# Single load buffers, the second batch's q transposed by DMA, and projections moved next to score bursts, in a Linformer attention with a gated feed-forward layer

## The chip, the cores and the metric

The kernel runs on one core of one Trainium2 chip. The metric is device microseconds of one launch, the median of several runs. The span is the time from the first to the last instruction in a profile of one of them, and the granted clock is the share of full speed at which TensorE was allowed to run. All runs told of here are of the fast state. Engines are named as in the profile: PE (TensorE), DVE (VectorE), ACT (ScalarE), POOL (GpSimd, which issues the loads here) and SP (SyncE, which issues stores and DMA transposes).

## The reference

Eight batches of eight heads, 1024 tokens, head size 64; keys and values are projected along the sequence to 64 rows, then softmax attention, then a feed-forward layer on 8192 tokens of width 512 with 2048 hidden units.

```python
k_proj = np.einsum('ks,bhsd->bhkd', E, k)
v_proj = np.einsum('ks,bhsd->bhkd', F, v)
scores = np.matmul(q, k_proj.transpose(0, 1, 3, 2)) / np.sqrt(64)
attn = softmax(scores)                    # over 64 columns
x = np.matmul(attn, v_proj)               # then (B, H, S, D) -> (B*S, H*D)
h = x @ w_in
out = (h * sigmoid(1.702 * h)) @ w_out
```

## The kernel before

The output is made in 16 blocks of 512 tokens, two a batch. In each block PE first runs 16 slots of `ffn1` (four matmuls each), then 8 slots of `ffn2` (eight matmuls each, named O to O+7). Attention work for later blocks is placed at fixed slots with `at(block, slot, ...)`: the projection of k and v of a batch, score bursts (four small matmuls of q with the projected k), and normalisation bursts. `qT` and `kt` are the transposed q and the transposed projected k that the scores read; `vq` is the projected v. The program fixes the order of the instructions itself (`manual_schedule`), so each engine has them in the order in which they are written; waits are put in where data or buffers ask for them. The listing is abridged.

```python
ldpool = ctx.enter_context(tc.tile_pool(name="ldpool", bufs=2))   # k, v, q as loaded

def load(b):                        # all on one in-order queue (POOL)
    load_kv(k, kt, b, "k_sb")
    if b == 1: load_kv(v, vt, b, "v_sb")
    load_q(b)                       # 8 pieces
    if b > 1:  load_kv(v, vt, b, "v_sb")

def proj(b):      # 16 matmuls in pairs: k into one half of a PSUM bank, v into the other
    ...
def kv_out(b):    # DVE copies k_b and the two vq; for b > 1 SP transposes k_b into kt by DMA
    ...
def q_tr(b, g):   # q on PE: 8 transposes, then one DVE copy    (batches 0 and 1)
    ...
def q_dma(b):     # q by one DMA transpose of 1 MB on SP        (batches 2 to 7)
    ...
# cut: prologue, four(), scores(), norm(), tok(), x_tr(), ffn1(), ffn2()
at(1, 4, proj(1)); at(1, 5, kv_out(1))
at(1, 7, lambda: k_tr(1, kbs[1], 0), q_dma(2))
for g in range(4):
    at(1, 8 + 2 * g, q_tr(1, g))
for b in range(2, B):
    j = max(2, NB2 * b - 3)         # NB2 = 2
    at(j, 2, proj(b)); at(j, 3, kv_out(b))
    if b > 2: at(NB2 * b - 4, O, q_dma(b))
for j in range(3, NBLK - 2):        # the bursts: scores and normalisation
    for u in range(2):
        if j + 3 < NBLK: at(j, O + 5 * u, scores(j + 3, u))
        at(j, O + 5 * u, norm(j + 2, u))
```

The softmax here doesn't subtract the row's maximum and nothing guards it: scores larger than these inputs give would overflow.

## Time and profile before

| | before |
|---|---|
| time, median of the first three runs | 518.31 us |
| span of the profiled run | 516.5 us, clock 1.000 |
| PE / DVE / ACT busy | 98% / 49% / 51% |
| start of block 1, 2, 3, 4 on PE (timeline) | 55.86, 91.14, 124.26, 156.25 us |
| last PE matmul starts | 512.64 us |

The prediction below shows the lines that carry the reading: PE is never idle after the first 22 us, so only what PE does, or waits for, sets the time. Starts are compared below rather than ends, because the ends of pipelined matmuls are modelled.

### The profile page before, as it was taken

The numbers are of one execution on the slowest core, as the hardware profiler recorded it, in microseconds if no ns is written. First come the engines' busy times: TensorE is split into PE (matmuls) and PEld (weight loads), VectorE is DVE, ScalarE is ACT, GpSimd is POOL, SyncE is SP. The second block draws the span as 40 slices with busy tenths as digits, with TensorE's granted clock in tenths as the row PEclk, the third lists the DMA queues.
The fourth block names the chain that finished last, engine by engine and source line by source line (L and its number), as shares of the span: only waits on it lengthen the run. The fifth ranks groups of instructions, "written<-read, shape, count | busy, mean of one in ns | idle before, by whom it ended". The sixth has DMA issues, their size and how long they took to land.

```text
span 516.5 us, 6729 instructions
## 1 busy us (share of the span) xinstructions
PE 506.9 (98%) x2856; PEld 233.2 (45%) x2856; DVE 251.4 (49%) x231; ACT 264.0 (51%) x439; POOL 77.4 (15%) x96
## 2 busy tenths in 40 slices
PE   6899999999999999999999999999999999999997
PEld 3584454444444444444444444444444444444444
DVE  3533324766774672818547282655818275560000
ACT  1575464555646456474555645465473646344351
POOL 6442620821510024000510000000000000000000
PEclk9999999999999999999999999999999999999999
DMA  9999999999996039550694201060200101010102
GB/s 162 197 203 207 217 180 182 165 191 159 241 152 162 1 90 166 106 133 0 147 176 121 53 41 48 0 164 0 84 4 1 81 1 81 1 82 1 81 1 82
DMA packets 113950, 53.78 MB, mean 104 GB/s; under 512 B 87680, under 2 KB 111488, under 8 KB 112000
## 3 DMA queue, kind: packets, MB, share of 16 engines
q0 software_dynamic: 84384, 29.37, 50.2%
q1 hardware_dynamic: 29456, 23.73, 16.6%
q8 instruction: 22, 0.36, 0.3%
q10 hardware_dynamic: 80, 0.26, 0.1%
q14 instruction: 8, 0.07, 0.0%
HBM read 59.24 MB, written 16.78 MB: 147 GB/s over the span
## 4 chain that ended last, share of the span: by engine, by line
PE 94%; DMA 4%; POOL 1%; issue 0%; DVE 0%; DVEq 0%; POOLq 0%
PE f_ps L333 43%; PE f_ps L301 42%; PE f_ps L144 3%; DMA w_in_sb<-in_moe_w_in_dram 2%; DMA v_sb<-in_v_dram 2%; PE f_ps L225 2%; PE d_ps L225 1%; PE n_ps L225 1%; PE f_ps L325 1%; PE n_ps L287 0%; PE d_ps L272 0%; PE f_ps L208 0%; POOL k_sb L57 0%; PE f_ps L205 0%; POOL q_sb L57 0%
## 5 line engine op out<-in xcount | busy, mean ns | idle before, releaser
L259 DVE RECIPROCAL rden<-d_ps 128x512 f32<-128x512 f32 x52 | 174.4, 3353 | 149.0 <-PE d_ps L225 149.0
L301 PE MATMUL f_ps<-xT,w_in_sb 128*128 128x512 bf16 (+1 forms) x1088 | 228.4, 367 | 0.2
L333 PE MATMUL f_ps<-w_out_sb,gT 128*128 128x512 bf16 x1008 | 227.0, 379 | 0.0
L304 ACT ACTIVATE gT<-f_ps 128x512 bf16<-128x512 f32 (+1 forms) x268 | 153.7, 575 | 85.4 <-PE f_ps L301 84.4
L301 PEld LDWEIGHTS <-w_in_sb 128*128 128x128 bf16 x1088 | 104.5, 98 | 116.4 <-issue 4.3
L333 PEld LDWEIGHTS <-gT 128*128 128x128 bf16 x1008 | 95.7, 98 | 120.4 <-issue 11.1
L336 ACT COPY o_sb<-f_ps 128x512 f32<-128x512 f32 x63 | 37.0, 587 | 133.5 <-PE f_ps L333 123.7
L63 POOL DMA_DIRECT2D q_sb<-in_q_dram x56 | 49.1, 894 | 67.5 <-DMA k_sb<-in_k_dram 27.7
L239 ACT ACTIVATE expT<-f_ps 128x512 bf16<-128x512 f32 (+1 forms) x68 | 35.2, 574 | 14.4 <-PE f_ps L225 14.4
L260 DVE TENSOR_TENSOR xT<-n_ps,rden 128x512 bf16<-128x512 f32 x52 | 36.0, 692 | 5.4
L327 DVE COPY o_sb<-f_ps 128x256 f32<-128x256 f32 x1 | 0.4, 424 | 50.9 <-PE f_ps L325 50.9
L57 POOL DMA_DIRECT2D k_sb<-in_k_dram x9 | 7.8, 864 | 103.7 <-PE f_ps L144 101.4
L239 ACT ACT_TABLE_LOAD x13 | 16.7, 1283 | 4.7 <-PE f_ps L225 4.5
L243 ACT ACT_TABLE_LOAD x14 | 18.0, 1283 | 0.3
L225 PE MATMUL f_ps<-qT,kt 64*64 64x512 bf16 (+1 forms) x136 | 13.8, 386 | 0.4 <-ACT expT L239 0.4
L144 PE MATMUL f_ps<-k_sb,eft 128*64 128x512 bf16 x56 | 13.4, 382 | 0.0
L144 PE MATMUL f_ps<-v_sb,eft 128*64 128x512 bf16 x56 | 13.4, 382 | 0.0
L211 DVE COPY qT<-f_ps 128x1024 bf16<-128x1024 bf16 x8 | 5.5, 692 | 12.4 <-PE f_ps L205 6.8
L277 DVE RECIPROCAL rd<-d_ps 128x4 f32<-128x4 f32 x22 | 3.8, 175 | 15.5 <-PE d_ps L272 15.4
L225 PEld LDWEIGHTS <-kt 64*64 64x64 bf16 x136 | 4.0, 103 | 14.3 <-issue 14.3
L225 PE MATMUL d_ps<-expT,ones 64*64 64x512 bf16 x104 | 10.2, 381 | 0.0
L225 PE MATMUL n_ps<-expT,vq 64*64 64x512 bf16 x104 | 10.0, 376 | 0.0
(57 smaller groups left out, 127.0 us busy)
## 6 DMA issues: line engine op xcount, KB each, us to landing
out_dram<-o_sb SPq DMA_DIRECT2D x15, 1024.0 KB, 4.5
k_sb<-in_k_dram POOLq DMA_DIRECT2D x7, 1024.0 KB, 13.5
v_sb<-in_v_dram POOLq DMA_DIRECT2D x7, 1024.0 KB, 10.7
q_sb<-in_q_dram POOLq DMA_DIRECT2D x56, 128.0 KB, 11.1
w_in_sb<-in_moe_w_in_dram POOLq DMA_DIRECT2D x8, 256.0 KB, 12.7
w_out_sb<-in_moe_w_out_dram POOLq DMA_DIRECT2D x4, 512.0 KB, 14.7
k_sb<-in_k_dram POOLq DMA_DIRECT2D x2, 512.0 KB, 8.0
out_dram<-o_sb SPq DMA_DIRECT2D x3, 256.0 KB, 2.0
```

The lines of the kernel that those rows point to most:

```text
L57: nc.gpsimd.dma_start(out=dst[b][:, h:h + n, js:js + jn], in_=sv[:, h:h + n, js:js + jn])
L63: nc.gpsimd.dma_start(out=qt[b][:, j], in_=qv[:, j])
L144: nc.tensor.matmul(kvps[b][r], eft[:, j, e * KP:(e + 1) * KP], (kt, vt)[e][b][:, :, j, :], start=(j == 0), stop=(j == J - 1))
L225: nc.tensor.matmul(outs[i][r], lhsTs[i][ri], rhss[i][ri], start=True, stop=True)
L239: nc.scalar.activation(expT[h][:, 2 * u + i, ts], s_ps[i], AF.Exp, scale=scale)
L243: nc.scalar.preload_act_table(AF.Gelu_apprx_sigmoid)
L259: nc.vector.reciprocal(rden, d_ps[i])
L260: nc.vector.tensor_tensor(x_of(h)[:, 2 * u + i, :], n_ps[i], rden, op=ALU.mult)
L301: nc.tensor.matmul(h_ps, w_in_sb[:, kc, fc * P:(fc + 1) * P], xT[j][:, kc, ts], start=(kc == 0), stop=(kc == KC - 1))
L304: nc.scalar.activation(gts[j][:, fc, ts], h_ps, AF.Gelu_apprx_sigmoid)
L333: nc.tensor.matmul(o_ps[n], gts[j][:, fc, n * P:(n + 1) * P], w_out_sb[:, fc, :], start=(fc == 0), stop=(fc == FC - 1))
L336: nc.scalar.copy(osb[j][:, n, :], o_ps.pop(n))
```

## The change

Its intent: PE no longer transposes q of batch 1, two half-size DMA transposes do; k, v and q have one buffer each, so that batch 2 is loaded only once batch 1 is used up and does not run beside those transposes; from batch 4 on the projection sits directly ahead of a burst, so that the array leaves its full tiling once instead of twice.

```diff
-    ldpool = ctx.enter_context(tc.tile_pool(name="ldpool", bufs=2))
+    ldpool = ctx.enter_context(tc.tile_pool(name="ldpool", bufs=1))
...
-    def q_dma(b):
+    def q_dma(b, j0=0, n=J):           # a part of q
...
     (prologue: tok(0, 0..1) ahead of the second v projection, x_tr spread out)
...
-    at(1, 4, proj(1))
-    at(1, 5, kv_out(1))
-    at(1, 7, lambda: k_tr(1, kbs[1], 0), q_dma(2))
-    for g in range(4):
-        at(1, 8 + 2 * g, q_tr(1, g))
+    at(1, 10, proj(1))
+    at(1, 11, kv_out(1))
+    at(1, 13, lambda: k_tr(1, kbs[1], 0))
+    at(1, 1, q_dma(1, 0, JB), q_dma(1, JB, JB))
...
+    at(1, O + 7, q_dma(2))
+    at(2, 2, proj(2))
+    at(2, 3, kv_out(2))
+    for b in range(3, B):
+        j = NB2 * b - 4
+        at(j, O, q_dma(b))
+        at(j, O + 6, proj(b), kv_out(b))
...
-                at(j, O + 5 * u, scores(j + 3, u))
-            at(j, O + 5 * u, norm(j + 2, u))
+                at(j, O + 6 * u, scores(j + 3, u))
+            at(j, O + 6 * u, norm(j + 2, u))
...
-            at(j, O + 6, gelu_table)
+            at(j, O + 7, gelu_table)
```

More of the change, by code (lines that the diff above doesn't have):

```diff
@@ L53, in load_kv @@
         if b not in dst:
-            dst[b] = ldpool.tile([P, H, J, D], BF16, name=name, bufs=1 if name == "q0_sb" else 2)
+            dst[b] = ldpool.tile([P, H, J, D], BF16, name=name)
         sv = src[b].rearrange("h (p j) d -> p h j d", p=P)
@@ L200, in go @@
             for jj in range(2):
-                j = 2 * g + jj
-                if b == 0:
-                    for h in range(H):
-                        r = h % 2 * D
-                        nc.tensor.transpose(t_ps[r:r + D, jj, h // 2, :], qt[0][:, h, j, :], ident)
-                else:
-                    for p in range(HP):
-                        nc.tensor.transpose(
-                            t_ps[:, jj, p, :],
-                            qt[b][:, j, 2 * p:2 * p + 2, :].rearrange("s t d -> s (t d)"), ident)
+                for h in range(H):
+                    r = h % 2 * D
+                    nc.tensor.transpose(t_ps[r:r + D, jj, h // 2, :], qt[0][:, h, 2 * g + jj, :], ident)
             nc.vector.tensor_copy(qT[b][:, 2 * g:2 * g + 2], t_ps)
         return go
-    def q_dma(b):
+    def q_dma(b, j0=0, n=J):
         def go():
-            qT[b] = att.tile([P, J, HP, P], BF16, name="qT")
-            nc.sync.dma_start_transpose(out=qT[b].rearrange("r j p s -> r (j p) s"),
-                                        in_=qt[b].rearrange("s j h d -> s (j h d)"))
+            if j0 == 0:
+                qT[b] = att.tile([P, J, HP, P], BF16, name="qT")
+            nc.sync.dma_start_transpose(out=qT[b][:, j0:j0 + n].rearrange("r j p s -> r (j p) s"),
+                                        in_=qt[b][:, j0:j0 + n].rearrange("s j h d -> s (j h d)"))
         return go
@@ L356 @@
         scores(0, u, 0)()
+    for p in range(2):
+        tok(0, p, 0)()
     v_out(0, proj0(1, 4, 2), 2, 1)
-    for p in range(3):
-        tok(0, p, 0)()
+    x_tr(0, 0, 0)()
     v_out(0, proj0(1, 6, 2), 3, 1, nc.scalar.copy)
-    for p in range(3):
-        x_tr(0, p, 0)()
+    tok(0, 2, 0)()
+    x_tr(0, 1, 0)()
     tok(0, 3, 0)()
+    x_tr(0, 2, 0)()
     q_tr(0, 1)()
@@ L396 @@
     at(2, 11, norm(3, 1))
-    for b in range(2, B):
-        j = max(2, NB2 * b - 3)
-        at(j, 2, proj(b))
-        at(j, 3, kv_out(b))
-        if b > 2:
-            at(NB2 * b - 4, O, q_dma(b))
     for j in (1, 2):
         at(j, O + 5, gelu_table)
+    at(1, O + 7, q_dma(2))
[5 more added lines that the diff above has]
+        at(j, O + 6, proj(b), kv_out(b))
     at(2, O + 5, norm(4, 0))
```

## The prediction

> **What bounds the kernel now.** I read the page first: the table of busy time, and the summary of the chain that ended last.
>
> ```profile
> PE 506.9 (98%) x2856; PEld 233.2 (45%) x2856; DVE 251.4 (49%) x231; ACT 264.0 (51%) x439; POOL 77.4 (15%) x96
> ...
> PE 94%; DMA 4%; POOL 1%; issue 0%; DVE 0%; DVEq 0%; POOLq 0%
> ```
>
> The reader is to see that TensorE (PE) is busy 98% of a span of 516.5 us and carries 94% of the chain; VectorE and ScalarE are half idle. Since a busy PE is not PE at its peak, I then read who waited for whom, for PE alone: its seven kinds of wait sum to 1.8 + 1.2 + 1.0 + 0.7 + 0.4 + 0.4 + 0.2 = 5.7 us, and the timeline puts all of them before 22 us. From 29.6 us to about 513 us the chain, in order of time, is PE only. So in that stretch a PE instruction removed is time removed, at its cost in the stream, and a PE wait added is time added. These are the pieces of the chain around the second batch's work in block 1, columns start, us, what:
>
> ```profile
> 60.34 1.85 PE f_ps L144 x16
> 62.18 2.70 PE f_ps L301 x12
> 64.88 0.22 PE f_ps L165 x4
> 65.10 0.97 PE f_ps L301 x4
> 66.07 0.45 PE f_ps L208 x8
> 66.52 1.73 PE f_ps L301 x8
> 68.24 0.45 PE f_ps L208 x8
> ...
> 73.90 1.73 PE f_ps L333 x8
> 75.62 0.34 PE f_ps L225 x4
> ```
>
> L208 is the transpose of q on PE (8 instructions in 0.45 us; they are to go), L144 the projection of k and v, L225 the score burst. A plain run gives the price of a 512-column matmul: 8 in 1.73 us, 0.216 us each. The projection is 8 concurrent pairs, 8 x 0.216 = 1.73, but takes 1.85: 0.12 us too much. The same on leaving: the run after it later in the trace, 52 of L301 in 11.33 us, has 11.33 - 52 x 0.2158 = 0.11 too much. A score burst of four concurrent matmuls takes 0.34 = 0.22 + 0.12, and the two bursts of the normalisation behind it take 0.22 each, with nothing on top. So changing the array's tiling costs about 0.12 going in and 0.11 coming out; staying in one costs nothing.
>
> **What the Trainium skill says.** "TensorEngine Tiling (Array Packing)", Key Properties: changing the tiling mode, not just the tile, drains TensorE. The 0.12 and 0.11 above agree. It also implies that going from the projection's tiling (128*64 in the groups) to the score burst's (64*64) is a change and drains too; no place of this trace has the two side by side, so that is open. "TensorE: Matmul & The Clock Gate", Back-to-back issue gap, gives N/2.4 + 2.5 ns, thus 56 ns at 128 columns; the trace's 0.45/8 = 56 ns agrees. The 219 ns "mean of one" of these transposes is latency, not their price. "DMA: Bandwidth & Descriptors", Issuing engines are not separate DMA queues: transfers issued from different engines share the same 16 DMA engines. The trace agrees: the whole-batch transpose of q took 14.78 us to issue and 21.1 us to landing at 104.4 us, beside loads, and 6.96 and 8.6 at 157.8 us, without them.
>
> **The change, part by part.**
>
> 1. *q of batch 1 by DMA.* Removed: 32 transposes on PE, 4 groups x 0.45 = 1.80 us, all on the chain; no tiling change sits beside them (the L301 runs after them take the plain 1.73). Four copies of qT on VectorE, 0.69 each, go too, worth nothing. The two DMA transposes are issued after the first slots of block 1, at about 57.5 us. The pieces of q land at 54.5 to 60.4 (eight issues between 32.2 and 53.9, with their landings). A half should cost 3.5 to 7 us of issue, half of 6.96 to 14.78, and about 1.6 more to land (8.6 - 6.96). So the first half is there by 62 to 67, the second by 68 to 73. Scores of block 2 need the first at 75.62 - 1.80 = 73.8, those of block 3 need the second at about 80. **Gain 1.8 us.**
>
> 2. *Projections beside bursts.* For batches 3 to 7 the projection moves to slot O+6 of block 2b-4, and for j of 3 and up the second burst moves there too. For batch 3 that is block 2, whose own bursts remain at O+5, so nothing merges. Batches 4 to 7 merge. Today each pays 4 changes, in and out twice, 0.46 us. Merged: 0.23 if going from 128*64 to 64*64 is free, 0.35 if it drains. **Gain 4 x 0.11 to 4 x 0.23 = 0.45 to 0.9 us; I take 0.6,** leaning to a drain there because the skill says so.
>
> 3. *Prologue reordered.* The first feed-forward matmuls pace on the landing of w_in: in PE's timeline they restart at 25.27, 26.61 and 27.95, and the chain names that DMA for 15.19 to 26.56. PE work moved ahead of that gains nothing as long as it ends by then. **Gain 0** (0.3 at most).
>
> 4. *One buffer each.* k of batch 2 now waits for the projection of batch 1 (slot 10 of block 1: 56.0 + 11 x 0.863 + 1.85 = 67.4), q of batch 2 for the landing of both transposes, v comes behind q in the same in-order queue. Whether this costs time is the real question. Undisturbed, a batch is loaded like this, columns start, us, engine, line, with waits in brackets:
>
> ```profile
> 190.53 0.88 POOL L57 DMA_DIRECT2D k_sb<-in_k_dram  x1 [45.54 <-PE f_ps L144]
> 191.40 6.14 POOL L63 DMA_DIRECT2D q_sb<-in_q_dram  x7
> 201.40 0.88 POOL L63 DMA_DIRECT2D q_sb<-in_q_dram  x1 [3.86 <-DMA k_sb<-in_k_dram]
> 202.60 0.88 POOL L57 DMA_DIRECT2D v_sb<-in_v_dram  x1 [0.32 <-issue]
> ```
>
> With v's 10.4 us to landing (DMA issues of this window) it is 202.60 + 10.4 - 190.53 = 22.5 us from k's issue to v's landing. So v of batch 2 lands at 67.5 + 22.4 = 89.9, or at about 91.5 if q has to wait until 73 (8 pieces of 0.88, then v). The projection of batch 2 comes at 94.55 today (the next L144 piece of the chain), so at 92.75: 1 to 3 us to spare. Next: q2 is transposed from about 90.5, to landing by 99 to 103, needed at 110.12 - 1.8 = 108.3: safe. The k transpose of batch 2 waits in the same queue; today it is issued at 102.23 and takes 6.9, ending 1.0 us ahead of its scores; it should keep that, unless q2's transpose holds the queue longer than about 10 us. Last: k3 is issued at 94.7, q3 from 99 to 103, v3 at 108 to 111, landing at 118.5 to 122; its projection, moved a block forward, comes at 122.7 - 1.8 = 120.9. That is a toss-up. From batch 4 on there are two blocks (61 us) for a load of 22.5. **Cost: I put 0.3, 0.2 and 0.4 on the three tight places, about 0.9 in all.**
>
> Sum: 518.31 - 1.8 - 0.6 + 0.9 = 516.8.
>
> **Rivals.**
>
> *The loads come late.* A wait of PE for v of batch 2 or 3, or for kt, takes the place of the transposes. For it: the slack of 1 to 3, 1.0 and about 0 us just worked out, and the profile's DMA row, near full until 170 us. Against it: the single buffers spread the loads, so those of batch 2 no longer fight those of batch 1, and the transposes should be nearer 7 than 14 us. If two places miss by 2 us, 518.5 and no gain; if each misses by 4, 524.
>
> *PSUM or VectorE becomes the wait at O+6.* There the projection's bank, two score banks and an open output bank are all four of that pool. For it: k_b and the two vq casts must free the bank, 0.68 + 2 x 0.43 = 1.5 us, before the next block's first matmul. Against it: between lie the burst (0.8) and eight L333 (1.8), and VectorE is done with the first burst's 2 x (3.35 + 0.69) = 8.1 us before the slot, some 13 us later. If wrong: 4 x 0.5 = 2 us, 518.8.
>
> *Everything is hidden, and drains are free between the two small tilings*: 1.8 + 0.9 and no cost: 515.6.
>
> **Range and chances.** The removed transposes are sure; the costs can only go up from 0. Best case 515.4 with 0.3 in the prologue, middle 516.8, and a late load pushes it to 518.5 or a little more. I say **516.8 us, 515.4 to 519.0**. A gain of 2% would need 10.4 us of PE work, and only about 2.7 leaves: chance 0.01. A loss of 2% needs stalls of 13 us: 0.02. Within 2%: 0.97.
>
> **What would show it right or wrong.** PE instructions must be 2856 - 32 = 2824, with no transpose of q after block 0. The chain should show, at each of blocks 4, 6, 8 and 10, a projection piece of 1.85 followed at once by score matmuls, of 0.34 if that drains and 0.22 if not. PE's waits should still sum to about 6 us: a wait by L144 for the DMA of v, or by L225 for qT or kt, between 90 and 125 us is the loads coming late; one by L301 for ScalarE or VectorE at a block's start is the PSUM rival. The first row of loads for batch 2 should be issued at 67 to 68 us. The prediction is wrong if batch 2 or 3 stalls for longer than the gains of 2.4 us, or if a wait that I have not seen, such as the q transposes running late in block 1, stops the score bursts there.

## The result, and the profile after

| | before | after |
|---|---|---|
| median of 6 runs each | 518.47 us (518.21 to 519.78) | 517.32 us (517.03 to 517.68) |
| ratio | | 0.9972, 95% interval 0.996 to 0.9985 |
| block 1 to block 2 (starts on PE) | 35.28 us | 33.49 us |
| block 2 to block 3 | 33.12 us | 36.98 us |
| block 3 to block 4 | 31.99 us | 30.05 us |
| block 4 to the last matmul | 356.39 us | 355.96 us |
| block 1 to the last matmul | 456.79 us | 456.49 us |

A ratio here is the mean time of one kernel's fast runs over that of the other's in the same rounds, so not quite the ratio of the medians. The changed kernel is about 0.3% faster in these rounds. From block 1 on the two traces differ by 0.30 us only; the medians differ by more because of the time before block 1, which varies from launch to launch: two of the six runs before (519.34 and 519.78) have a long start, and none of the six after has (see the word on noise below).

The page of the changed kernel, busy times and the summary of the chain that ended last, against the same two lines of before in the prediction:

```profile
PE 505.4 (98%) x2824; PEld 232.3 (45%) x2824; DVE 248.4 (48%) x227; ACT 262.6 (51%) x439; POOL 77.3 (15%) x96
...
PE 90%; DMA 6%; POOL 1%; DVE 1%; ACT 1%; issue 0%; POOLq 0%; DVEq 0%; ACTq 0%
```

The 32 transposes are gone from PE (2856 to 2824), but its share of the chain fell from 94 to 90% and the DMA share rose: somewhere PE is no longer what sets the time. The chain in order of time (start, us, what) says where:

```profile
87.55 1.73 PE f_ps L327 x8
89.27 1.35 PE f_ps L295 x7
90.62 13.32 DMA qT<-q_sb
104.01 0.49 issue
104.50 3.70 POOL q_sb L63 x5
108.19 0.63 issue
108.82 0.71 POOL q_sb L63
109.69 1.73 POOL q_sb L63 x2
111.42 11.07 DMA v_sb<-in_v_dram
122.53 1.89 PE f_ps L144 x15
```

Read it from the bottom. The projection of batch 3 (L144) goes on at 122.53, when the load of v has landed. That load was issued at 111.42, behind the eight pieces of q. Those were issued from 104.50 on, when the transpose of batch 2's q had landed and given up the only q buffer. And that transpose was issued at 90.62, just after the store of block 1. PE's own timeline shows what this costs (start, us, engine, line, operation; the wait in brackets):

```profile
120.60 0.40 PE L144 MATMUL f_ps<-k_sb,eft 128*64 128x512 bf16 x1
122.53 0.38 PE L144 MATMUL f_ps<-v_sb,eft 128*64 128x512 bf16 x1 [1.53 <-DMA v_sb<-in_v_dram]
122.54 0.40 PE L144 MATMUL f_ps<-k_sb,eft 128*64 128x512 bf16 x1
```

k and v matmuls of a pair normally start together. Here v's starts 1.93 us after k's, so about 1.9 us are lost; the bracket says 1.53, because it counts from the modelled end of the k matmul. The queue of loads shows the same two waits from its own side:

```profile
94.67 0.88 POOL L57 DMA_DIRECT2D k_sb<-in_k_dram  x1 [14.12 <-PE f_ps L144]
104.50 7.00 POOL L63 DMA_DIRECT2D q_sb<-in_q_dram  x8 [8.95 <-DMA qT<-q_sb]
111.42 0.94 POOL L57 DMA_DIRECT2D v_sb<-in_v_dram  x1
```

v's buffer was free from 94.67 on, as k's was. The issue of k ended at 95.55, so v lost 15.9 us by standing behind q.

The merged projections, here that of batch 4 in the chain of the changed kernel:

```profile
183.08 1.85 PE f_ps L144 x16
184.92 0.34 PE f_ps L219 x4
185.26 0.22 PE d_ps L219 x4
```

The scores (L219) follow at once, but take 0.34 us and not the 0.22 of the burst after them: the change between the two small tilings costs 0.12 us too.

So the account of the two traces is: from block 1 to block 2, 33.49 - 35.28 = -1.79 us, the transposes. From block 2 to 3, 36.98 - 33.12 = +3.86, and from 3 to 4, 30.05 - 31.99 = -1.94: the projection of batch 3 has moved one block ahead (1.85 and 0.11 for the way out, 1.96), and the 1.9 left over is the wait. From block 4 on, -0.43, four merges. In sum -0.30.

### The profile page after: what moved, and what is told of

It is laid out like the page before. It is cut to its first block, busy times and chain, and to the rows that moved or that the text cites. A ratio compares the mean times of both kernels' runs of the same rounds, so it can differ in the third digit from the quotient of the medians.

```text
span 515.9 us, 6686 instructions
## 1 busy us (share of the span) xinstructions
PE 505.4 (98%) x2824; PEld 232.3 (45%) x2824; DVE 248.4 (48%) x227; ACT 262.6 (51%) x439; POOL 77.3 (15%) x96
## 4 chain that ended last, share of the span: by engine, by line
PE 90%; DMA 6%; POOL 1%; DVE 1%; ACT 1%; issue 0%; POOLq 0%; DVEq 0%; ACTq 0%
PE f_ps L327 40%; PE f_ps L295 40%; DMA qT<-q_sb 3%; PE f_ps L144 2%; DMA v_sb<-in_v_dram 2%; PE f_ps L219 2%; POOL q_sb L63 1%; PE d_ps L219 1%; DMA ef_f<-in_E_dram 1%; PE n_ps L219 1%; PE f_ps L319 1%; PE n_ps L281 1%; PE f_ps L123 1%; PE f_ps L152 1%; PE d_ps L266 0%
## 5 line engine op out<-in xcount | busy, mean ns | idle before, releaser
L298 ACT ACTIVATE gT<-f_ps 128x512 bf16<-128x512 f32 (+1 forms) x268 | 151.3, 575 | 63.0 <-PE f_ps L295 62.0
L188 DVE CAST k_b<-f_ps 64x512 bf16<-64x512 f32 x7 | 4.8, 680 | 30.1 <-PE f_ps L144 30.1
L144 PE MATMUL f_ps<-v_sb,eft 128*64 128x512 bf16 x56 | 13.4, 381 | 1.5 <-DMA v_sb<-in_v_dram 1.5
L219 PE MATMUL f_ps<-qT,kt 64*64 64x512 bf16 (+1 forms) x136 | 13.8, 386 | 0.4 <-ACT expT L233 0.4
L144 PE MATMUL f_ps<-k_sb,eft 128*64 128x512 bf16 x56 | 13.6, 382 | 0.0
L219 PEld LDWEIGHTS <-kt 64*64 64x64 bf16 x136 | 4.0, 103 | 14.3 <-issue 14.2
L219 PE MATMUL d_ps<-expT,ones 64*64 64x512 bf16 x104 | 10.2, 381 | 0.0
L219 PE MATMUL n_ps<-expT,vq 64*64 64x512 bf16 x104 | 10.0, 376 | 0.0
```

What stands on the lines that cost most here:

```text
L144: nc.tensor.matmul(kvps[b][r], eft[:, j, e * KP:(e + 1) * KP], (kt, vt)[e][b][:, :, j, :], start=(j == 0), stop=(j == J - 1))
L219: nc.tensor.matmul(outs[i][r], lhsTs[i][ri], rhss[i][ri], start=True, stop=True)
L298: nc.scalar.activation(gts[j][:, fc, ts], h_ps, AF.Gelu_apprx_sigmoid)
```

## The experiments

Theory: the transposes are worth 1.8 us and the merges 0.42, and one wait, for v of batch 3, takes back 1.9; its cause is the order of waits in two queues. Rivals: that the loss is spread over slower transfers; that it is a matter of bandwidth; that the buffers themselves make the gain or the loss.

A word on noise. The time up to block 1 differs from launch to launch: in the traces block 1 starts between 55.4 and 57.5 us. Where it starts after 56.8 (e2, e3, e4, e6, e7, e8), PE waits 2.3 to 2.8 us in all for the first loads (k and v, or E and F through ACT); in the other traces it waits 0.9 to 2.0 us. In four of those six (e3, e4, e6, e7) the granted clock is also 0.50 for 3.41 us between 7 and 15 us; in the other traces it is 1.00 there.

The mean clock of every run is on record, and it sorts the times. Of 104 runs of the kernel before in the three sessions, the 34 with a mean clock of 0.995 to 0.997 took 519.29 us or more; of the 70 at 0.999 or 1.000 all but six took under 518.6. How many runs of a version fall among the slower ones differs (18 of 22 in e3, none in e1), so the medians of all runs partly compare starts. Therefore I give beside each the median of the runs at 0.999 or more, and the stretch from the start of block 1 to the start of the last matmul in its one trace, which leaves the start out. For e1, e2 and e7, which from block 1 on differ only in the order of two loads or the place of one projection, the stretches agree to 0.01 us. The runs e5 to e8 are from a second chip; there the kernel before has 517.91 us at full clock, against 517.90 and 518.06 on the first. All versions passed the comparison with the reference. Each is timed in five rounds.

| run | median us | ratio to before | at full clock: median us (runs) | block 1 to last matmul |
|---|---|---|---|---|
| before | 518.47 | | 517.93 (70 of 104) | 456.79 |
| changed | 517.32 | 0.9972 | 517.32 (6 of 6) | 456.49 |
| e0_after, the changed kernel again | 517.74 | 0.9983 | 517.38 (8 of 14) | 456.81 |
| e1_proj3_later | 515.60 | 0.9935 | 515.60 (6 of 6) | 454.58 |
| e2_v3_first | 515.88 | 0.9943 | 515.88 (6 of 6) | 454.58 |
| e3_two_buffers | 519.86 | 1.0025 | 518.43 (4 of 22) | 456.58 |
| e4_not_merged | 516.60 | 0.9958 | 515.95 (4 of 8) | 455.00 |
| e5_q1_on_pe | 517.41 | 0.9990 | 517.39 (11 of 14) | 456.37 |
| e6_q2_earlier | 516.57 | 0.9970 | 516.19 (15 of 22) | 454.72 |
| e7_old_prologue | 515.80 | 0.9959 | 515.70 (15 of 19) | 454.58 |
| e8_all_merged | 517.98 | 0.9997 | 517.94 (13 of 14) | 456.88 |
| e9_two_buffers_q2_earlier | 515.72 | 0.9949 | 515.72 (6 of 6) | 454.84 |

### Is the wait there each time? The changed kernel again

> The changed kernel once more, unaltered, on the chip of the next run, to have its spread and a second trace. Theory: PE waits again for v of batch 3 at the second matmul of batch 3's projection, 1 to 3 us by run; about 1.7 us slower than the version with that projection moved back (515.6), so 517.3. Rival (the wait in the first trace was chance): no wait in this trace and times of 515.6 to 516.

Measured: 517.74 us (516.90 to 519.07, 14 runs). The wait is in this trace too, and longer: the v matmul starts at 123.61 and its k partner at 121.35, 2.26 us apart, and the stretch is 456.81 us. The wait stands in both traces of this kernel.

### Take the wait away by moving its reader: e1_proj3_later

```diff
-        at(j, O + 6, proj(b), kv_out(b))
+        if b == 3:
+            at(3, 2, proj(b))
+            at(3, 3, kv_out(b))
+        else:
+            at(j, O + 6, proj(b), kv_out(b))
```

> The changed kernel with one thing undone: the projection of batch 3 goes back from slot O+6 of block 2 to slot 2 of block 3, where the kernel before has it. My theory: the wait of the first v matmul for the load of v (PE at a standstill, second matmul of the pair 1.93 us late at 122.53) is the whole of the loss, so it goes and nothing takes its place: about 1.9 us less than the changed kernel's 517.3 (515.4), ratio to the kernel before 0.9935 to 0.9945, end of the last PE matmul about 1.9 us earlier than 512.4 in the trace. Rival (a loss spread over slower transfers and the tail of block 1, of which the wait is only the visible part, or a wait that moves to kt or qT of batch 3): less than 1 us gained, and a new PE wait at block 3.

Measured: 515.60 us (515.36 to 515.76), the stretch 454.58, which is 1.91 less than in the changed kernel's trace and 2.23 less than in its second one: just the two waits. No new wait on PE appears. The rival of a spread loss falls. This version has the lowest median of all (e2, e7 and e9 lie within 0.3 us of it) and beats both kernels.

### Take it away by the order of the queue: e2_v3_first and e6_q2_earlier

In the first, v of batch 3 is loaded ahead of q (`if b in (1, 3)` instead of `if b == 1`). In the second, all is as changed but for one slot:

```diff
-    at(1, O + 7, q_dma(2))
+    at(1, O + 5, q_dma(2))
```

> The changed kernel with v of batch 3 loaded ahead of q instead of behind it; the projection stays in block 2. My theory: v comes late because it stands in the in-order load queue behind q of batch 3, which can't be issued before the transpose of q of batch 2 has landed (103.94); v itself has a free buffer from 94.7 on. Then v is issued at about 95.6 and landed by 108, the wait at 122.5 is gone and the time is that of the run with the later projection, about 515.4. Rival (the load queue is limited by what the 16 DMA engines move, so any order is late): v lands after 118 all the same or the transposes of q become late, and the time stays at 516.5 or more.

> The changed kernel with one edit: the transpose of q of batch 2 stands two slots earlier in the SyncE queue (O+5 of block 1), so before the store of block 1 and not behind it; the projection of batch 3 stays in block 2 and v behind q. Theory: q2 lands at 85, so the transpose is issued at 85 instead of 90.6 and landed by about 97 instead of 103.9; q3 follows it, v3 behind q3, all some 6 us earlier: v3 lands at about 116.5, before PE gets to it at 120.6, and the wait of 1.9 us is gone: 454.6 from block 1 to the last matmul, 515.4 to 515.8 in all. Rival (v3 is late because of bandwidth, not because of this chain of waits): the wait remains above 1 us.

Measured: with v first, v is issued at 96.78 and landed at 114.21, long before its reader; no wait, 515.88 us, a stretch of 454.58 as in e1. The projection is still in block 2, so its place did no harm once the load came in time. The landing came 6 us later than I had put it, without harm. The queue of loads in this trace, k and then v of batch 3:

```profile
95.90 0.88 POOL L57 DMA_DIRECT2D k_sb<-in_k_dram  x1 [13.73 <-PE f_ps L144]
96.78 0.88 POOL L57 DMA_DIRECT2D v_sb<-in_v_dram  x1
```

With the transpose two slots earlier the trace has no wait either (454.72), but the median, 516.57, falls only by part, and the runs spread from 515.39 to 518.30. The trace shows why a wait in other runs is likely: the transpose was issued at 86.95 and landed at 95.80, yet v landed only at 120.74, with block 1 starting at 57.19. Counted from block 1 that is 63.6 us, against 66.9 in the changed kernel, and PE comes to it at 65.0. A slack of 1.4 us is less than the launches differ by. That the wait comes back in some of these runs I infer; only one was profiled. The start alone does not explain the spread: 15 of the 22 runs have the full clock, and they still reach from 515.39 to 517.09. I had expected 6 us of gain in the landing and got 3.3.

### Are the single buffers needed? e3_two_buffers and e9_two_buffers_q2_earlier

The first gives the pool its two buffers back and leaves all else; the second also issues the transpose of batch 2's q at O+5.

> The changed kernel with two buffers each for k, v and q of batches 1 and up, as in the kernel before; all else as changed. My theory: batch 3 is loaded a batch earlier, so the v wait of 1.9 us goes; but the loads of batch 2 then run beside the two transposes of q of batch 1, which issue in 5.4 and 1.5 us in the changed kernel and would take up to 7 each; the second is still needed only at about 80. I expect 515.4 to 516.0, no PE wait of the second half's scores. Rival (one buffer is there because the transposes of q under load come late): the scores of block 2 or 3 in block 1 (73.6 and 79.9) wait 1 to 4 us for qT, and the time is 517 to 519.

> Two buffers each again, as in the run that came out slower (519.9), but with the transpose of q of batch 2 two slots earlier in the SyncE queue. Theory: what was slow there was one wait, kt of batch 2 (scores 1.9 us late in its trace) standing in the queue behind that transpose, whose issue took 11.85 us beside the loads; issued at about 85 it is out of the way at 97, before k_b is ready at about 102, so the wait goes, and the time falls from 519.9 to 515.6 to 516.5. Rival (with two buffers the transfers under load are late whatever their order): still over 517.5, with a wait for kt or qT at another place.

Measured: with two buffers alone it took 519.86 us, against my expectation. That this is more than the kernel before is in good part the start: the stretch is 456.58, 0.2 less than before; at full clock it is 518.43 against 517.90, from four runs only; and 18 of the 22 runs are at a mean clock of 0.993 to 0.997, against 14 of the 29 of the kernel before in the same rounds. Against e1 the stretch is 2.0 us longer, and that is the wait shown below. The halves of q of batch 1 did come later (issued in 8.0 and 7.3 us, landed at 74.25 and 79.72), but in time. The wait is at a third place, here the queue of SP (start, us, line, operation) in the trace of e3_two_buffers:

```profile
91.19 0.34 SPq L334 DMA_DIRECT2D out_dram<-o_sb  x1
91.88 11.85 SPq L211 DMA_TRANSPOSE qT<-q_sb  x1
103.78 1.25 SPq L190 DMA_TRANSPOSE kt<-k_b  x1
```

and PE's waits in the same trace:

```profile
PE f_ps L219 <- DMA kt<-k_b: 1.9, 1, 1.9
```

Beside the last loads of batch 3 and the first of batch 4, the transpose of q takes 11.85 us to issue, and the small transpose of k_b stands behind it until 103.78, lands at 111.24, and the scores wait 1.9 us. In the changed kernel, with loads held back by the single buffer, the same transpose issues in 7.14 us and kt is issued as soon as DVE is done:

```profile
90.62 7.14 SPq L211 DMA_TRANSPOSE qT<-q_sb  x1
100.21 1.29 SPq L190 DMA_TRANSPOSE kt<-k_b  x1
```

With two buffers and the transpose ahead of the store, kt is issued at 100.31 in the trace of e9:

```profile
57.25 40.48 SPq L211 DMA_TRANSPOSE qT<-q_sb  x3
97.79 0.58 SPq L334 DMA_DIRECT2D out_dram<-o_sb  x1
100.31 1.19 SPq L190 DMA_TRANSPOSE kt<-k_b  x1
```

and the time is 515.72 us (515.50 to 516.48), within noise of the best. So the single buffers are not what is fast. They keep the loads off the transposes, which hides a badly placed instruction in the SP queue; placed better, two buffers do as well. What stays open: the 22 runs of e3 go up to 522.8 us, and its one trace explains 2.0 of the 4.3 us that its median lies above e1 (2.8 at full clock, but from four runs); 1.2 more in the profiled run is the start, and the rest can't be seen in it.

### The merges alone: e4_not_merged, against e1

Projections of batches 3 to 7 and the second bursts go back to where the kernel before has them.

> The changed kernel with the projections of batches 3 to 7 and the second burst of each block back where the kernel before has them; q of batch 1 by DMA and the single buffers stay. Against the run with only batch 3's projection moved back this undoes the merging alone. My theory, from the trace (0.34 us for the scores after a projection, so the array still drains there): each of four merges saves one change in and out less one drain, 0.11 us, so this is 0.42 us slower than that run: about 515.8. Rival (the merge saves the whole pair of changes, 0.23 each, or also some waits of other engines): 0.9 us slower, 516.3; or none: 515.4.

Measured: the stretch is 455.00 against 454.58, 0.42 us for four merges, 0.105 each. The median is 516.60, but four of its eight runs (515.93 to 516.11) are at full clock, with a median 0.35 above e1, and four (517.09 to 518.07) at a mean clock of 0.997. One change of four is saved at each merge, as the 0.34 in the trace said.

### The transposes alone: e5_q1_on_pe, against e1

The four `q_tr(1, g)` of the kernel before stand in for the two `q_dma(1, ...)`.

> The version with batch 3's projection moved back (no PE wait), with q of batch 1 transposed by 32 matmuls on PE in block 1 again; single buffers and merges stay. Theory: the removed transposes are worth exactly their 4 x 0.45 = 1.8 us, so from the start of block 1 to the last matmul 456.4 instead of 454.6, and about 517.4 in all. Rival (the DMA transposes cost something back through the loads that they delay, or the single buffers alone bring the gain): under 1.2 us between the two, or over 2.4.

Measured: 517.41 us, a stretch of 456.37, 1.79 more than e1, and 1.79 between the medians at full clock. The DMA transposes cost nothing back in this setting.

### The prologue alone: e7_old_prologue, against e1

> The version with batch 3's projection moved back, with the prologue's order of tok and x_tr as in the kernel before. Theory: PE is paced by the landing of w_in there, the reordering is worth 0 to 0.3 us, so 515.6 to 515.9; the start varies by over 1 us from launch to launch anyway, so likely not to be told from nothing. Rival (the reordering is worth as much as PE's waits in the prologue, 0.5 us and more): over 516.1.

Measured: 515.80 us (515.59 to 517.87) against 515.60: 0.1 at full clock, nothing that could be told from the spread of the start.

### All projections beside bursts: e8_all_merged

```diff
-    at(2, 1, norm(3, 0))
-    at(2, 2, proj(2))
-    at(2, 3, kv_out(2))
+    at(2, 2, proj(2), kv_out(2), norm(3, 0))
+    at(2, O + 5, proj(3), kv_out(3))      # ahead of scores(5, 1) and norm(4, 0)
```

together with the two edits to the queues (v of batch 3 first, q of batch 2 at O+5).

> Everything together: the changed kernel, v of batch 3 loaded ahead of q, the transpose of q of batch 2 two slots earlier, the projection of batch 3 beside the burst at O+5 of block 2 and that of batch 2 beside the first burst of block 2, so that all projections from batch 2 on sit next to a burst. Theory: no PE wait for a load, and two more merges at 0.105 us each against the version with the later projection: 454.4 from block 1 to the last matmul, about 515.4 in all. Rival (a wait takes the merges' place: kt or a PSUM bank in block 2): 454.6 or more.

Measured: 517.98 us, a stretch of 456.88: a miss, 2.3 us worse than e1. The chain of this trace turns onto DVE right behind the moved projection:

```profile
93.30 1.89 PE f_ps L144 x16
95.22 0.68 DVE k_b L188
95.93 0.43 DVE vq L182
96.38 0.43 DVE vq L182
96.83 3.37 DVE rden L253
100.30 0.69 DVE xT L254
100.99 3.28 DVE rden L253
104.36 0.70 DVE xT L254
105.10 0.40 PE n_ps L219 x2
```

The three copies of the projection now run ahead of the normalisation, which itself starts later; the next burst (slot 11) needs the PSUM banks that this normalisation is still reading (PE waits 0.6 us for the reciprocals and 0.8 for the products, beside shorter waits), and PE goes on only at 105.10. The same happens at 132.56. Two merges worth 0.2 us cost some 2.5. DVE, half idle on average, is the bound for these two stretches. This is read from the one trace; no run moves the normalisation back ahead of the copies alone. The two edits to the queues are unlikely to be the cause, since each of them alone brought no wait (e2, e6).

## Why the prediction was right or wrong, point by point

The time, 517.32 us, lies in the stated range of 515.4 to 519.0 and 0.5 above the 516.8 stated. Counted as a gain, 1.5 us was foretold and 1.15 is the difference of the medians. That these two are so near is in part luck. Three of the four parts act from block 1 on; there 1.5 us less was foretold, and the two traces of the changed kernel have 0.30 less and 0.02 more than the one before. The rest of the 1.15 is not in these stretches; most of it must come from the start, where the prediction put a gain of 0 and the launches differ by more than that.

1. *q of batch 1 by DMA, 1.8 us:* right. e5 against e1 has 1.79. The halves landed at 64.41 and 68.12, inside the windows given (62 to 67, 68 to 73).
2. *Projections beside bursts, 0.45 to 0.9, taken as 0.6:* the mechanism was right and the term too big; it measured 0.42. I leaned to a drain between the two small tilings, for which my own sum was 0.45, and still put the middle towards there being none. The trace shows 0.34 after each of the four projections, as with a drain.
3. *Prologue, 0:* right as far as e7 can tell.
4. *One buffer each, 0.9 us in all:* this is the step that was mis-sized. Of the three tight places, v of batch 2 landed at 90.43 (put at 89.9) and was needed at 92.5; kt landed at 106.95, ahead of its scores at 108.0 by 1.1; both cost nothing. The third, the "toss-up", cost 1.9 and 2.3 us in two traces instead of 0.4. Two things made this term too small. I averaged over hit and miss, where a wait once there costs its full length: the late end of my own window, 122 against a reader at 120.9, was a wait of 1.1. And I took a transpose to land 1.6 us after its issue ended, from one that ran alone. Here it was issued in 7.14 us but landed 13.3 us after its start, at 103.94, not 99 to 103, with a store (issued at 89.92) and a load (94.67) beside it; in e6, issued ahead of both, it landed after 8.9 us. Everything behind it in the load queue moved with it, and v landed at 122.49, past the end of the window of 118.5 to 122.

Two slips in the recorded text: two misses of 2 us are 518.31 - 1.8 - 0.6 + 4 = 519.9, outside the stated range, and not the 518.5 given under the first rival; and the DMA row is full until 155 us, not 170 (six tenths in the slice after that).

The rival "the loads come late" therefore came true at one of the places that it named, and ate nearly the whole of the gain. The rival of PSUM and DVE at O+6 did not: no PE wait for ACT or DVE at the start of blocks 4, 6, 8 or 10. A wait of the same kind came in e8, where the normalisation was put behind a projection.

## What to carry to other kernels

When one engine is the bound, moving work off it can pay what that work takes in its stream (1.79 us here, 1.80 foretold), but only if no transfer behind the move comes late; follow each in-order queue by hand and write down what stands ahead of the transfer that PE will want first. A free buffer is of no use to a load that stands behind one which waits for its own, and here one buffer was enough when the order was right: reordering (v ahead of q, or one transpose two slots earlier) did what buffers were meant to do. Where the slack comes out smaller than the spread between launches, don't put work there to save a tenth of a microsecond: moving one projection back by a block was worth 1.9 us, all the merges together 0.42.

## What the Trainium skill lacked or had wrong

- "TensorEngine Tiling (Array Packing)", Key Properties, is right that changing the mode drains TensorE, but has no figure. Here a change costs 0.12 us going in and 0.11 coming out, and 0.12 from 128*64 to 64*64, so that putting two small tilings side by side saves one change of four, 0.105 us.
- "DMA: Bandwidth & Descriptors", DMA Transpose (X-bar), says which engines may issue a transpose, but not how long it holds the issuing queue; elsewhere the page has a bandwidth for it and sequencer cycles of "previous generations", but no time for one beside loads. Here the 1 MB transpose of q of batch 2 took 6.84 to 7.21 us to issue in the runs with single buffers, and 1 MB transposes beside double-buffered loads (before, e3, e9) took 11.85 to 15.05 us. From issue to landing it was 8.6 us alone and 13.3 us beside a load and a store. What stands behind it in that queue waits, 1.9 us of PE in e3.
- The same page, Rules for kernel authors, advises to issue a DMA early and to wait late. It does not say that in an in-order load queue a load whose buffer is free is held by an earlier one whose buffer is not: v was held 15.9 us.
- On the price of a transpose in a busy stream, "TensorE: Matmul & The Clock Gate", Part 4, gives durations, some 275 ns in one kernel and 390 ns alone. What PE lost by them in this stream was 1.79 us for 32, 56 ns each. The same page, Back-to-back issue gap, has this figure for a single matmul of 128 columns, but about 81 ns for a stream of weight loads and matmuls, and 131 ns at 512 columns. Here, with a weight load for every matmul, it was 56 and 216 ns in the stream.
